# A short convolution with k as the stationary operand, and the second half of a fused kernel brought into one written-out order

## The chip, the cores and the metric

The kernel runs on one core of one Trainium2 chip. The metric is the device time of one execution in microseconds, the median of several runs. Lower is better.

## The reference

The input `A_q` (2048 x 640, time by channels) passes through two blocks with residuals, both conditioned by `c`. Cut to what matters:

```python
def _A_ref(q, k, v, shift_k, ssm_k, ssm_D):          # 2048 x 640, ks = 4
    k_pad = jnp.pad(k, ((0, 0), (ks - 1, 0), (0, 0)))
    for t in range(ks):                              # short convolution, per channel
        k_shift = k_shift + k_pad[:, t:t + S, :] * shift_k[:, ks - 1 - t]
    kv = k_shift * v
    y = irfft(rfft(kv, 2 * S) * rfft(ssm_k, 2 * S))[:S]   # long convolution, per channel
    return q * (y + kv * ssm_D)

def _B_ref(x, w_in, w_sp, b_sp, w_out):              # Fh = 864
    z = gelu(x @ w_in)                               # 2048 x 1728
    z1, z2 = z[..., :Fh], layernorm(z[..., Fh:])
    g = w_sp @ z2 + b_sp                             # w_sp mixes over time, 2048 x 2048
    return (z1 * g) @ w_out

sa, ca, ga, sb, cb, gb = split(silu(c) @ w_mod)      # 6 x 640
x = x + ga * _A_ref(layernorm(x) * (1 + ca) + sa, k, v, ...)
x = x + gb * _B_ref(layernorm(x) * (1 + cb) + sb, ...)
```

## The kernel before

Data and matrices are bf16, sums in PSUM are fp32. There are 16 time tiles of 128 rows and five "units" of 128 channels each.

**Short convolution** (`load_kv`, `short_conv`, L512 to L559). For each unit the DMA brings k and v transposed, channels on the partitions and time along the row (`big`, 128 x 4096). `dg` holds four 128 x 128 diagonal matrices with the four taps. `taps` runs 16 matmuls per unit, all at L245: `dg` is stationary, 512 columns of k, shifted by 0 to 3, move. `times_v` (L553, DVE) multiplies the PSUM tile `sm` by v in place. `kvw` (L559, on SP's queue) writes the unit's 512 KB into a DRAM scratch array `kv_scr`, and `load_X` (L390) reads it back in the layout that the transform wants: the 16 time blocks times 8 channels of a group on the partitions. This is the tile `X` of the input side (XU). The filter `ssm_k` comes into the same layout straight from DRAM (XK), and DVE adds `ssm_D` to one column of it (L400).

**Long convolution.** It is a transform by matmuls. Per unit: stage 1 multiplies `X` by a small table `F1bd`; ACT or DVE casts the result to X1 (L248); `forward` multiplies by `M`; DVE multiplies input and filter spectra (`Tf` or `T`, L462), POOL or DVE adds the real and imaginary products (`W`, L476); `inv` multiplies by `G`; the casts `Z<-pz` follow; a transfer turns Z (`ZT<-Z`, L685); a last small stage with `Ebd` gives y, which is multiplied by the normed x (`gh`, L678) and added to `xt` (L698). The layer norm of x takes its statistics on DVE (L580) or on ACT (L576, L577) and is applied on DVE, ACT or POOL (L606 to L610).

**gMLP.** Norm and modulation of the new x (Z, L843 to L897), z = gelu(x w_in) by 320 matmuls of 432 columns, then the spatial mix. It treats time tiles p and p+8 as a pair (p = 0..7). Each pair takes seven block products (`ps`, L1013) of 8 matmuls x 432 columns instead of eight. Their stationary sides are blocks of w_sp (`wT`) or sums of these (`S`, L988, DVE). DVE and ACT add them up into two tiles u (L1030 to L1047; `keep` on ACT, L1019 and L1021). Each u is turned by a DMA (`uT<-u`, L1052). `project_pair` (L1181 to L1225) multiplies a pair of uT by `w_o` in the same seven-block way: 25 matmuls of 320 columns in pieces (L1179), with sums of uT (`R`, POOL, L1171) and of w_o (`V`, L1161 and L1235), and partial rows `O` that ACT copies and POOL and DVE add up. `project` (L1140) does one tile directly with 14 matmuls.

**What sets the order.** Each engine works through its own list in program order; nothing is scheduled on the chip. Up to the first mix pair (p = 0) the program is a plan: the code registers operations with their dependences (`Plan.op`), and the string `ORDER` gives the order in which they are issued and which engine takes each where there is a choice ("D0 D13 ... S88 A1 P1032": engine letter and operation number). `SLOTS` gives the number of buffers of each pool tag. `FILLS` and `MODE` are further tables of it. After the plan the rest is issued as the code is written, in the loop over p = 1..7 (L1237): the products of pair p, with the projection of pair p-1 put between and behind them in four parts (`begin`, `most`, `sums`, `end`). Pairs 0 to 6 go through `project_pair`; tiles 7 and 15 go through `project` at the very end. SP issues nearly all DMAs, in order: when one of them has to wait for its data, all behind it wait too.

## Time and profile before

| quantity | value |
|---|---|
| median of 3 runs | 311.58 us (310.77 to 313.09) |
| profiled execution, its own time | 310.85 us |
| its span, first to last instruction | 309.1 us |
| granted TensorE clock | 1.00 throughout |
| PE busy | 293.9 us (95%), 2485 matmuls |
| DVE busy | 270.7 us (88%) |
| ACT / POOL busy | 166.6 us (54%) / 181.2 us (59%) |
| DMA | 45.23 MB, queue 1 at 68.1% of 16 engines |

The span has two stages. Up to about 133 us runs the plan's transform stage, where all engines and the DMA are busy at once; the first modulation `Z<-s` of the gMLP input on DVE (L871) starts at 133.03 us and the first matmul of z at 133.48 us. From there PE does z, the mix and the projection. "Busy" counts an engine's instructions without the time it waits; PE's matmuls are pipelined, so that the duration of one (346 ns at 432 columns) is longer than the distance from one to the next. A row of the view of groups reads: line, engine, operation, output and inputs, shapes, count, then busy us and mean ns of one, then the idle time of the engine just before them with what ended it.

### The profile page before, as it was taken

What the parts mean: (1) busy time and instruction counts of PE and PEld (TensorE: products, weight loads), DVE (VectorE), ACT (ScalarE), POOL (GpSimd) and SP (SyncE); (2) the same over time, 40 slices, a digit from 0 to 9 for tenths busy, and PEclk for the clock granted to TensorE, in tenths of its full rate; (3) what the DMA queues carried; (4) which work ended last, traced back from release to release, by engine and by line L of the source; (5) the groups of instructions that cost most, each with busy time, mean ns of one, the idle gap of its engine ahead of it and who ended that gap; (6) DMA issues with size and microseconds to landing.
All of it is one profiled execution on the core that took longest, in us unless ns stands there. A gap on an engine that the chain in (4) does not pass through costs nothing.

```text
span 309.1 us, 6509 instructions
## 1 busy us (share of the span) xinstructions
PE 293.9 (95%) x2485; PEld 195.3 (63%) x2485; DVE 270.7 (88%) x523; ACT 166.6 (54%) x302; POOL 181.2 (59%) x208
## 2 busy tenths in 40 slices
PE   7988989989999998989999999999999999999995
PEld 2765678867889998645555555555555555565554
DVE  8898998979998988998897998998999878888574
ACT  6988699978888957547676688141111111021110
POOL 2542877838988999555423612039858475673922
PEclk9999999999999999999999999999999999999999
DMA  8999899998995849404679910073477593730323
GB/s 177 210 227 253 231 305 224 220 190 196 225 223 113 203 84 298 152 2 95 127 146 237 204 3 0 2 127 70 89 152 165 120 192 73 167 81 21 83 55 111
DMA packets 127954, 45.23 MB, mean 146 GB/s; under 512 B 117071, under 2 KB 127156, under 8 KB 127924
## 3 DMA queue, kind: packets, MB, share of 16 engines
q1 hardware_dynamic: 127770, 44.78, 68.1%
q8 instruction: 19, 0.31, 0.4%
q14 instruction: 11, 0.09, 0.1%
q10 hardware_dynamic: 154, 0.05, 0.1%
HBM read 16.11 MB, written 5.24 MB: 69 GB/s over the span
## 4 chain that ended last, share of the span: by engine, by line
PE 47%; DVE 12%; issue 1%; POOL 1%; DMA 1%; ACT 1%; DVEq 0%; POOLq 0%
PE ps L1013 21%; PE pu L245 8%; PE pz L245 8%; PE po L1179 6%; DVE st L704 2%; PE pz L1013 1%; PE po L1140 1%; DVE Tf L462 1%; DMA uT<-u 1%; DVE T L462 1%; DVE xt L698 1%; PE pu L1013 1%; DVE u L1041 1%; DVE T L998 1%; DVE gh L746 1%
## 5 line engine op out<-in xcount | busy, mean ns | idle before, releaser
L245 PEld LDWEIGHTS <-Z 128*128 128x128 bf16 x320 | 31.2, 98 | 28.1 <-DVE Z L871 1.3
L245 PE MATMUL pu<-X,M 128*128 128x128 bf16 (+1 forms) x480 | 45.8, 237 | 2.3 <-DVE Tf L462 1.9
L245 PEld LDWEIGHTS <-M 128*128 128x128 bf16 x480 | 37.4, 98 | 8.8 <-issue 3.2
L476 POOL TENSOR_TENSOR W<-Tf 128x256 bf16<-128x256 f32 x47 | 34.7, 760 | 11.6 <-DVE Tf L462 8.3
L1013 PEld LDWEIGHTS <-S 128*128 128x128 bf16 x256 | 25.0, 98 | 21.6 <-issue 0.5
L245 PE MATMUL pz<-big,Z 128*128 128x432 bf16 x160 | 33.1, 346 | 0.8 <-DVE Z L871 0.8
L248 ACT CAST X<-s 128x1024 bf16<-128x1024 f32 x31 | 31.9, 1028 | 2.5 <-PE s L245 2.3
L245 PE MATMUL pu<-big,Z 128*128 128x432 bf16 x160 | 32.5, 346 | 0.0
L462 DVE TENSOR_TENSOR Tf<-pu,KH 128x1024 f32<-128x1024 f32 x25 | 30.3, 1219 | 2.4 <-PE pu L245 1.2
L1197 ACT COPY O<-po 128x320 f32<-128x320 f32 x7 | 3.0, 427 | 54.4 <-PE po L1179 54.4
L1013 PEld LDWEIGHTS <-wT 128*128 128x128 bf16 x192 | 18.8, 98 | 16.6 <-issue 1.0
L245 PEld LDWEIGHTS <-G 128*128 128x128 bf16 x330 | 24.7, 98 | 2.0 <-issue 0.2
L248 ACT CAST KH<-pu 128x512 bf16<-128x512 f32 x40 | 23.0, 600 | 5.1 <-PE pu L245 5.1
L248 ACT CAST Z<-pz 128x512 bf16<-128x512 f32 x38 | 22.3, 601 | 5.3 <-PE pz L245 5.1
L245 PEld LDWEIGHTS <-X 128*128 128x128 bf16 x288 | 18.1, 97 | 7.6 <-DMA X<-kv_scr 2.3
L1013 PE MATMUL ps<-X,wT 128*128 128x432 bf16 x112 | 22.7, 346 | 0.0
L1013 PE MATMUL ps<-T,S 128*128 128x432 bf16 x112 | 22.7, 346 | 0.0
L1200 POOL TENSOR_TENSOR O<-O,xt 128x320 f32<-128x320 f32 x7 | 6.4, 908 | 27.7 <-ACT O L1199 27.7
L1013 PE MATMUL ps<-X,S 128*128 128x432 bf16 x112 | 21.6, 346 | 0.0
L245 PE MATMUL s<-F1bd,X 128*128 128x256 bf16 x128 | 19.2, 272 | 2.2 <-DVE X L400 1.2
L245 PE MATMUL sm<-big,dg 128*128 128x512 bf16 (+1 forms) x80 | 20.4, 379 | 0.0
L926 DVE BATCH_NORM_STATS2 stz<-X 128x6 f32<-128x432 bf16 x32 | 18.1, 591 | 0.9 <-ACT X L920 0.7
(205 smaller groups left out, 664.3 us busy)
## 6 DMA issues: line engine op xcount, KB each, us to landing
wm<-in_w_mod_dram SPq DMA_DIRECT2D x6, 800.0 KB, 6.0
xt<-in_A_q_dram SPq DMA_DIRECT2D x4, 640.0 KB, 6.2
out_dram<-ot SPq DMA_DIRECT2D x15, 160.0 KB, 2.4
big<-in_B_w_in_dram SPq DMA_DIRECT2D x2, 1080.0 KB, 9.2
X<-in_A_ssm_k_dram SPq DMA_DIRECT2D x4, 512.0 KB, 5.2
kv_scr<-big SPq DMA_DIRECT2D x4, 512.0 KB, 3.5
X<-kv_scr SPq DMA_DIRECT2D x4, 512.0 KB, 4.8
w_o<-in_B_w_out_dram SPq DMA_DIRECT2D x6, 160.0 KB, 3.1
```

Of the source, the lines that this page charges most:

```text
L245: nc.tensor.matmul(o, lhsT=w, rhs=x, start=start, stop=stop)
L248: (e.copy if e is nc.scalar else e.tensor_copy)(dst, src)
L462: e.tensor_tensor(T_[:], (tl[pu] if src is None else tl[src])[:, :, :, None, :].to_broadcast(shape), tl[KH][:, :, None, :, :].to_broadcast ...
L476: e.tensor_tensor(tl[W][:, :, o, :], T_[:, :, 0, o, :], T_[:, :, 1, 1 - o, :], op=ALU.add if o else ALU.subtract)
L698: op("GD" if u < NU - 1 else "D", "res", lambda e: e.tensor_tensor(sl, sl, gl, op=ALU.add), r=[("gh", (u, g))], w=[("xt", (u, n)) for n in ...
L704: op("D", "ln2", lambda e, n=n: e.bn_stats(out=st2[:, n, (0, 0, 0, 1, 2)[u], :], in_=xt[:, n, us[0] * DU:(u + 1) * DU]), r=[("xt", (v, n)) ...
L746: op("D", "yml", lambda e, ghv=ghv, py=py, i0=i0, k=k: e.tensor_tensor(ghv, ghv, tl[py][:, i0:i0 + k], op=ALU.mult), r=[py], w=[("gh", (u, ...
L926: op("D", "stz", lambda e, i=i, n=n, fc=fc: e.bn_stats(out=stz[:, n, fc, :], in_=tl[z2][:, i, fc * FC:(fc + 1) * FC]), r=[(z2, (i, fc))], ...
L998: nc.vector.tensor_tensor(y if o is None else T[o][:, sl, :], x, y, op=ALU.subtract)
L1013: nc.tensor.matmul(ps[:, :FC], lhsT=lhs[:, s_, :], rhs=rhs(s_), start=(s_ == 0 and not more), stop=(s_ == HT - 1), skip_group_check=more)
L1179: nc.tensor.matmul(ps[:, :HS], lhsT=w(k), rhs=x(k), start=start and k == 0, stop=stop and k == n - 1, skip_group_check=True)
L1200: nc.gpsimd.tensor_tensor(m5, m5, x_of(1, 1), op=ALU.add)
```

## The change

Two things change at once, with one new `ORDER` for everything.

*Short convolution.* k still comes transposed, now with 16 columns of zeros ahead of it (`KPAD`, a memset). The operands change places: a 128-column slice of k, shifted by 0 to 3, is stationary, and a 128 x 128 `dg` moves. The result has time on the partitions and channels along the row. A unit takes 16 x 4 = 64 matmuls of 128 columns instead of 16 of 512; that makes 320 in place of 80. v is loaded as it lies in DRAM, without a transpose: unit 0 alone in two halves, then units 1 and 2 as one transfer of 1 MB, then 3 and 4. `times_v` (now L610) writes to a new tile in Z's pool, in the order (c n g). One transposing transfer from SBUF to SBUF (`regroup`, L625) turns that into XU. The scratch array in DRAM, its six writes and its six reads are gone. XU's rows come in another order (n, g), so stage 1 gets a second table `F1ng` for it, with one more small mask, one more set of index bits, and one more cosine on ACT.

*The rest in the plan.* Everything behind the first mix pair is now registered in the plan as well (1438 operations in `ORDER`). The sums S, V, R and O and the multiplications by z1 (`lsm`, `c22b`, `c22m`) may stand on DVE or POOL; some u multiplications thus go to POOL. `c22` and `last_sum` are split into separate operations. `PAIRS` is (1, ..., 6): tiles 0 and 8 are projected directly, with 28 matmuls instead of 25 and without R and O for that pair. Pieces of the projection and products of later pairs alternate piece by piece. `SLOTS` is extended by the tags of the mix.

```diff
 FILLS = (4, 6, 2, 2, 4, 3, )
+PAIRS = (1, 2, 3, 4, 5, 6)
-SLOTS = dict(Tf=2, W=2, X=3, X1=4, KH=9, T=3, Z=3, ZT=1, wm=1, big=2, dg=2, st1=2, s1=1, sm=2, pu=2, pz=2)
+SLOTS = dict(Tf=2, W=2, X=3, X1=4, KH=9, T=3, Z=3, ZT=1, wm=1, big=2, dg=2, st1=2, s1=1, sm=2, pu=2, pz=2,
+             wT=6, S0=2, S1=2, S2=2, S3=2, mm=4, o=4, m1=1, m5=1, ms=1, c22=1, c=1, u0=2, u1=2, uT=4, R=2, ot=3,
+             O0=1, O1=1, O2=1, O3=1, O4=1, O5=1)
-D0 D13 D100 G101 S88 A1 P1032 P7 A4 A10 G5 A23 D15 D102 D109 D103 D110 A112 D115 A111 S2 D6 P1033 P8 A11 D14 A16 D116
+G5 D13 D101 D0 D14 A1 G102 S525 D103 S2 D116 D15 P7 A10 S23 D104 S83 S84 S26 G122 D117 G6 A4 P1034 A38 S24 D18 A532 P8
...
-                        mm(ps[i // k][:, i % k, :], tl[X][:, cp + i, :], F1flat, True, True)
+                        mm(ps[i // k][:, i % k, :], tl[X][:, cp + i, :], F1flat[X[1]], True, True)
...
-        SCH = 512
-                e.dma_start_transpose(tl[name][:, o + h * m:o + (h + 1) * m], src[0, h * m:(h + 1) * m, dt * P:(dt + 1) * P])
+        KPAD = 16
+        SCH = 4
+        GROUP = {0: (0,), 1: (1, 2), 3: (3, 4)}
+                    e.dma_start_transpose(k_of(u)[:, KPAD + h * m:KPAD + (h + 1) * m], A_k[0, h * m:(h + 1) * m, u * DU:(u + 1) * DU])
+            op("DG", "kpad", lambda e: e.memset(k_of(u)[:, 0:KPAD], 0.0), r=[(name, "new")], w=[(name, ("k", j, "pad"))])
+                    e.dma_start(v_of(0, ns.start, NT // n) if u0 == 0 else tl[name][:], v_nat[:, ns, ds])
...
-                    p_ = new(ps, "sm", [P, SCH], F32)
-                    for j in range(4):
-                        lo = 0 if i else j
-                        mm(p_[:, lo:], tl[dg][:, j, :], tl[name][:, i * SCH - j + lo:(i + 1) * SCH - j], j == 0, j == 3)
+                    p_ = new(ps, "sm", [P, SCH, DU], F32)
+                    for m in range(SCH):
+                        t0 = KPAD + (i * SCH + m) * P
+                        for j in range(4):
+                            mm(p_[:, m, :], k_of(u)[:, t0 - j:t0 - j + P], tl[dg][:, j, :], j == 0, j == 3)
...
-                    e.tensor_tensor(vsl, tl[ps][:], vsl, op=ALU.mult)
+                    dst = tl[kvt][:].rearrange("p c (n g) -> p n c g", g=8)[:, i * SCH:(i + 1) * SCH]
+                    e.tensor_tensor(dst, tl[ps][:].rearrange("p n (c g) -> p n c g", g=8),
+                                    v_of(u, i * SCH, SCH).rearrange("p n (c g) -> p n c g", g=8), op=ALU.mult)
...
-                op("S", "kvw", lambda e, sl=sl: e.dma_start(kv_scr[dt * P:(dt + 1) * P, sl],
-                                                                   tl[name][:, S + sl.start:S + sl.stop]),
+                    e.dma_start_transpose(tl[name][:, cs, :], tl[kvt][:, cs, :].rearrange("p c q -> p (c q)"))
+                op("S", "kvt", fn, r=[kvt] + ([(name, "new")] if h else []), w=[(name, h)] + ([] if h else [(name, "new")]),
...
-                late("D", "lastsum", lambda: last_sum(0, "d", 0, 1), r=["paird", "s1", "bcol", ("z1", (0, 1))], w=[("u", 0)])
+                    late("D", "lsa", lambda e: last_sum(e, p, "d", 0), r=[pair["d"], s1_, "bcol"], w=["cd_%d" % p], new=[("cd_%d" % p, "c")])
+                    late("DG", "lsm", lambda e: last_sum(e, p, "d", 1), r=["cd_%d" % p, ("z1", (p, 1)), (U[0], "new")], w=[(U[0], 1)])
...
-    for p in range(1, HT):
-        nxt = p + 1 < HT
-        product(p, 1, bank)
...
-    project(HT - 1)
-    end()
-    project(NT - 1)
+        for p in range(HT):
+            if p in PAIRS:
+                project_pair(p)
+            else:
+                project(p)
+                project(p + HT)
+        plan.run({"P": nc.tensor, "A": nc.scalar, "D": nc.vector, "G": nc.gpsimd, "S": nc.sync})
```

The order moves instructions on every engine. Three places follow. In the rows the number at the end of a name counts tiles and differs between the two kernels.

First, SP's queue in the first quarter of the program (`xt` is a part of x, `wm` of w_mod). Before:

```order
9 L566 DMA xt_68<-in_A_q_dram 128x4x640
10 L521 DMA_TRANSPOSE big_334<-in_A_k_dram 128x2048
11 L559 DMA kv_scr_134<-big_207 128x1024 x2
12 L754 DMA KH_385<-in_c_dram 5x128
13 L521 DMA_TRANSPOSE big_334<-in_A_v_dram 128x2048
14 L390 DMA X_483<-kv_scr_134 128x8x128 x2
15 L566 DMA xt_68<-in_A_q_dram 128x4x640
16 L521 DMA_TRANSPOSE big_575<-in_A_k_dram 128x2048
17 L521 DMA_TRANSPOSE big_575<-in_A_v_dram 128x2048
18 L559 DMA kv_scr_134<-big_334 128x2048
```

After:

```order
8 L820 DMA KH_243<-in_c_dram 5x128
9 L632 DMA xt_66<-in_A_q_dram 128x4x640
10 L417 DMA X_383<-in_A_ssm_k_dram 128x16x128
11 L625 DMA_TRANSPOSE X_414<-Z_284 128x8x128 x2
12 L564 DMA_TRANSPOSE big_492<-in_A_k_dram 128x2048
13 L632 DMA xt_66<-in_A_q_dram 128x4x640
14 L579 DMA ZT_531<-in_A_v_dram 128x16x256
15 L564 DMA_TRANSPOSE big_492<-in_A_k_dram 128x2048
16 L632 DMA xt_66<-in_A_q_dram 128x4x640
17 L686 DMA wm_664<-in_w_mod_dram 128x5x640
18 L625 DMA_TRANSPOSE X_854<-Z_593 128x16x128
```

The write and read of the scratch array (rows 11 and 14, then 18) became one row per unit, the transposing regroup (rows 11 and 18); v's transposing loads became plain ones, and the loads of x moved relative to them.

Second, the start of ACT's list (`gh` and `sums` are the layer norm's statistics of x, `M2` the forward matrix, `X1` the cast of the first stage). Before:

```order
4 L248 COPY sk_102<-sm_158 128x4x5
5 L536 ACTIVATE dg_167<-ident_73,sk_102 128x128 x4
6 L348 ACTIVATE M2_80<-T_174,mturn_125 128x4x64 x2
7 L248 CAST D_col_101<-sm_196 128x80
8 L255 ACTIVATE f1c_122<-f1i_123,mpi_118 128x32
9 L348 ACTIVATE M2_80<-T_182,mturn_125 128x4x64 x2
10 L348 ACTIVATE M2_80<-T_177,mturn_125 128x4x64 x2
11 L248 CAST X1_238<-pz_239 128x2x32x8
```

After:

```order
6 L591 ACTIVATE dg_190<-ident_71,sk_101 128x128 x4
7 L642 ACTIVATE gh_93,sums_108<-xt_66 128x640
8 L643 ACTIVATE gh_93,sums_108<-xt_66 128x640
9 L272 CAST D_col_100<-sm_206 128x80
10 L375 ACTIVATE M2_78<-T_158,mturn_125 128x4x64 x2
11 L279 ACTIVATE f1c_122<-f1i_123,mpi_118 128x32
12 L642 ACTIVATE gh_93,sums_108<-xt_66 128x640
13 L643 ACTIVATE gh_93,sums_108<-xt_66 128x640
14 L375 ACTIVATE M2_78<-T_177,mturn_125 128x4x64 x2
15 L272 CAST X1_259<-pz_260 128x2x32x8
```

Two tiles' statistics of x now stand ahead of the first cast of X1, the first of them ahead of the sines for M2.

Third, the end of DVE's list (`u2`, `u3` are the last pair's u, tiles 7 and 15; L1142, and L1310 after, close the direct projection of a tile). Before:

```order
443 L1041 TENSOR_TENSOR u3_2791<-c22_4325,G2_81 128x432
444 L1046 SCALAR_TENSOR_TENSOR c_4343<-ps_4279,bcol_2787,s1_4314 128x432
445 L1047 TENSOR_TENSOR u2_2790<-c_4343,G2_81 128x432
446 L1046 SCALAR_TENSOR_TENSOR c_4356<-ps_4316,bcol_2787,s1_4314 128x432
447 L1047 TENSOR_TENSOR u3_2791<-c_4356,G2_81 128x432
448 L1204 TENSOR_TENSOR O_3422<-po_4333,O_3422 128x320
449 L1212 TENSOR_TENSOR ot_4329<-po_4331,xt_68 128x320
450 L1217 TENSOR_TENSOR ot_4330<-po_4334,O_3422 128x320
451 L1218 TENSOR_TENSOR ot_4329<-po_4332,O_3422 128x320
452 L1142 TENSOR_TENSOR ot_4393<-po_4394,xt_68 128x320
```

After:

```order
433 L1122 SCALAR_TENSOR_TENSOR c_4582<-ps_4510,bcol_3033,s1_4508 128x432
434 L1124 TENSOR_TENSOR u2_3036<-c_4582,G2_79 128x432
435 L1122 SCALAR_TENSOR_TENSOR c_4593<-ps_4541,bcol_3033,s1_4508 128x432
436 L1350 TENSOR_TENSOR ot_4567<-po_4521,O_3919 128x320
437 L1344 TENSOR_TENSOR O_3919<-po_4595,O_3919 128x320
438 L1344 TENSOR_TENSOR O_3919<-O_3919 128x320
439 L1350 TENSOR_TENSOR ot_4615<-po_4610,O_3919 128x320
440 L1350 TENSOR_TENSOR ot_4617<-po_4577,xt_66 128x320
441 L1350 TENSOR_TENSOR ot_4617<-po_4550,O_3919 128x320
442 L1350 TENSOR_TENSOR ot_4615<-po_4610,O_3919 128x320
443 L1310 TENSOR_TENSOR ot_4666<-po_4639,xt_66 128x320
```

The two multiplications that finish u3 have left DVE for POOL, and the last pair projection is closed entirely behind the last product's sums; on PE 26 matmuls of pairs 5 and 6 now stand between the last product and tile 7.

665 lines of the change are left out of this document (378 added, 287 removed).

## Prediction

> **What bounds the kernel now.** I read the table of windows first, cut where the program changes its nature: at 133 us, where the gMLP's input begins, and at 205 us, where the mix from pair 1 on begins. Its columns are busy us and count for PE, PEld, DVE, ACT and POOL, then the granted clock, the DMA share and GB/s.
>
> ```profile
> 0.00:133.00 133.00, 123.71 (x1497) 99.74 (x1497) 120.82 (x225) 107.51 (x192) 92.20 (x118) 1.00 0.93 205
> 133.00:205.00 72.00, 70.70 (x390) 37.63 (x391) 65.35 (x170) 44.99 (x83) 23.90 (x31) 1.00 0.48 93
> 205.00:309.00 104.00, 99.44 (x600) 57.96 (x598) 84.50 (x130) 14.10 (x29) 65.09 (x60) 1.00 0.52 108
> ```
>
> The clock is full everywhere, so it explains nothing. In the first stage PE (123.7 of 133 us) and DVE (120.8) are both nearly full and feed each other; DMA is at 0.93. The stage can be shortened by about 9 us at most without taking work from PE. Behind 133 us PE alone sets the pace, and there only its gaps can be won. Next come the waits of DVE and PE, and those of SP's queue (us in total, times, longest):
>
> ```profile
> DVE X L400 <- DMA X<-in_A_ssm_k_dram: 1.9, 1, 1.9
> DVE st L580 <- DMA xt<-in_A_q_dram: 1.0, 1, 1.0
> DVE X L248 <- PE pz L245: 0.7, 1, 0.7
> DVE big L553 <- DMA big<-in_A_v_dram: 0.3, 1, 0.3
> ...
> PE pz L245 <- DMA X<-kv_scr: 1.5, 1, 1.5
> ...
> SPq L390 <- DMA kv_scr<-big: 9.3, 4, 3.7
> ```
>
> DVE's waits for loads are 1.9, 1.0 and 0.3 us. Its wait of 0.7 us for `pz` is one for a load too: that first-stage result was late because PE had waited 1.5 us for the read of the scratch array. Together they are 3.9 us of DVE's 12.2 idle us in this stage. The last row is the round trip at work: the read stands in SP's queue until the write has landed, 9.3 us in all, and every load behind it is late by that. The late `ssm_k` load is one that stands in this queue.
>
> **The taps.** Four starts of PE rows give the distance from one matmul to the next, two for 512 columns with `dg` stationary, two for 128 columns with a stationary of their own each:
>
> ```profile
> 24.45 1.03 PE L245 MATMUL sm<-big,dg 128*128 128x512 bf16 x4
> 25.32 0.38 PE L245 MATMUL pz<-F1bd,X 128*128 128x256 bf16 x2
> ...
> 123.20 0.61 PE L721 MATMUL pu<-ident,Z 128*128 128x128 bf16 x8
> 123.65 0.61 PE L721 MATMUL pz<-ident,Z 128*128 128x128 bf16 x8
> ```
>
> At 512 columns it is 0.87/4 = 217 ns, at 128 it is 0.45/8 = 56 ns. 80 x 217 = 17.4 us go and 320 x 56 = 17.9 us come: +0.5 us of PE in a stage where PE is idle for 9.3 us, so nothing on the path. The risk is the weight load, of which there are now 320 in place of 80. One lasts 98 ns, longer than the matmul that it belongs to:
>
> ```profile
> L245 PEld LDWEIGHTS <-M 128*128 128x128 bf16 x480 | 37.4, 98 | 8.8 <-issue 3.2
> ...
> 63.53 1.05 PE L245 MATMUL pu<-X,M 128*128 128x256 bf16 x12
> 64.41 0.60 PE L245 MATMUL s<-F1bd,X 128*128 128x256 bf16 x4
> ```
>
> But twelve matmuls, eight of 128 and four of 256 columns, each with a load of its own, take 0.88 us from start to start: with 98 ns each they could not be under 1.18 us. The loads overlap, and the stream runs at the rate of its columns. So the cost is between +0.5 us (56 ns) and +14 us (320 x 98 = 31.4 us against 17.4); I take +0.5, since two rows of this form stand there.
>
> The Trainium skill speaks against this. Its page "TensorE: Matmul & The Clock Gate", section "Back-to-back issue gap", gives for a long stream of pairs of weight load and matmul about 81 ns at 128 columns and 131 ns at 512, and calls the 56 ns that of an isolated matmul. By it the taps would go from 10.5 us to 25.9 us, +15 us of PE. This trace agrees with neither figure (56 and 217 ns), though no row has 16 such matmuls on odd column offsets of the stationary.
>
> **The regroup.** It takes the place of a write, a wait and a read. Median us from issue to landing:
>
> ```profile
> kv_scr<-big SPq DMA_DIRECT2D x4, 512.0 KB, 3.5
> X<-kv_scr SPq DMA_DIRECT2D x4, 512.0 KB, 4.8
> ...
> uT<-u SPq DMA_TRANSPOSE x16, 3.0
> ...
> ZT<-Z SPq DMA_TRANSPOSE x4, 8.3
> ```
>
> Write and read take 8.3 us. The trace has no transposing SBUF transfer of this size; the nearest are uT (7 blocks of 128 columns, 3.0 us) and ZT (32 blocks, 8.3 us). With 16 blocks the regroup lies between them, by blocks at 3.0 + 9 x 0.21 = 4.9 us. XU is thus there some 3.4 us earlier after its last multiplication by v, between 0 and 5.3 us, and SP is free of the blocked read. I take the 3.9 us of DVE's waits as gone; the bounds are 0 (they come back as other waits) and 3.9.
>
> **DVE's and POOL's work in the first stage.** The multiplication by v now reads v from another tile and writes in strides; its rows and those of the work that the order moves onto DVE or off it:
>
> ```profile
> L553 DVE TENSOR_TENSOR big<-sm,big 128x512 bf16<-128x512 f32 x20 | 13.4, 684 | 1.0 <-PE sm L245 0.6 <-DMA big<-in_A_v_dram 0.3
> ...
> L1041 DVE TENSOR_TENSOR u<-c,G 128x432 bf16<-128x432 f32 x8 | 6.5, 818 | 0.3
> ...
> L248 DVE CAST Z<-pz 128x512 bf16<-128x512 f32 x2 | 1.4, 676 | 0.0
> L476 DVE TENSOR_TENSOR W<-Tf 128x256 bf16<-128x256 f32 x3 | 1.3, 441 | 0.1
> L580 DVE BATCH_NORM_STATS2 st<-xt 128x6 f32<-128x320 bf16 x16 | 6.9, 472 | 1.0 <-DMA xt<-in_A_q_dram 1.0
> L610 DVE TENSOR_SCALAR gh<-xt,mv,rstd 128x640 bf16<-128x640 bf16 x4 | 2.3, 599 | 0.0
> ```
>
> The cast to Z writes a transposed order too and takes 676 ns, as the multiplication before: I take 684 again, +0. The slowest row of two operands with an fp32 source, 818 ns for 432 columns (L1041), would make it 970 ns, +5.7 us over 20. By the order DVE gains four casts to Z (2.7 us) and four sums W (1.8), and loses four statistics (1.9) and three applications of the norm (1.8): +0.8 us. What DVE loses goes to ACT and POOL, which have 25 and 41 us idle in this stage; the second F1 table and the zero columns are a few tenths on engines that wait at the start anyway.
>
> **ACT's start.** Here the order costs something. Rows of before, and what the moved statistics last (L576 and L577 are two instructions per tile, 738 ns each):
>
> ```profile
> 4.03 1.28 ACT L536 ACTIVATE dg<-ident,sk 128x128 bf16<-128x128 bf16 x4
> ...
> 8.64 0.59 ACT L248 CAST X<-pz 128x512 bf16<-128x512 f32 x1
> ...
> L576 ACT ACTIVATE gh<-xt 128x640 bf16<-128x640 bf16 x8 | 5.9, 738 | 2.5 <-DMA xt<-in_A_q_dram 2.5
> ...
> xt<-in_A_q_dram SPq DMA_DIRECT2D x4, 640.0 KB, 6.2
> ...
> 0.72 0.46 SPq L390 DMA_DIRECT2D X<-in_A_ssm_k_dram  x1
> ```
>
> The first load of x is now SP's first, in the place of the last row, and lands at about 0.7 + 6.2 = 6.9 us; ACT, whose taps matrices are done at 5.3, waits 1.6 us for it, and then works through two tiles' statistics (4 x 0.738 = 2.9 us) ahead of the first cast of X1. That cast moves from 8.64 to about 13 us, +4.4. Queued behind it are the sines of `M`, the other casts, and `KH`, for which the first product waits. DVE has index work, statistics and multiplications by v to do meanwhile, so the cost is between 0 and +4.4 us; I take +2.5.
>
> First stage: -3.9 + 2.5 + 0.8 = **-0.6 us**.
>
> **The second half.** PE's gaps behind 133 us: in the windows at the top it lacks 1.3 us up to 205 and 4.6 behind that. Of these 4.6 the last 2.9 are the end, when PE is done and the output is written. So 3.0 us of gaps are to be won. The largest that the timeline shows, and the transfer that the last one waits for:
>
> ```profile
> 222.58 0.70 PE L1179 MATMUL po<-V,uT 128*128 128x320 bf16 x4 [0.44 <-DVE ot L1217]
> ...
> 228.38 1.62 PE L1013 MATMUL ps<-T,wT 128*128 128x432 bf16 x8 [0.71 <-DVE c L1039]
> ...
> 301.64 2.08 PE L1140 MATMUL po<-w_o,uT 128*128 128x320 bf16 x14 [0.61 <-DMA uT<-u]
> ...
> 230.00 2.86 PE po L1179 x21
> ...
> 243.63 2.86 PE po L1179 x21
> ...
> 298.62 2.98 DMA uT<-u
> ...
> L1206 POOL TENSOR_TENSOR O<-O,xt 128x320 f32<-128x320 f32 x7 | 8.2, 1178 | 0.0
> L1200 POOL TENSOR_TENSOR O<-O,xt 128x320 f32<-128x320 f32 x7 | 6.4, 908 | 27.7 <-ACT O L1199 27.7
> ```
>
> The 0.44 us belongs to pair 0's projection, which came late because POOL first had to make V; now pair 0 takes no V at all, and V has the round of a pair (243.63 - 230.00 = 13.6 us) more. The 0.71 us is DVE's, behind sums S that may now go to POOL. The 0.61 us is the end: the turned u of tile 7 takes 2.98 us, and before only the 21 pieces of pair 6 (2.86 us, so 0.136 each) covered it. Now 26 pieces lie between the last product and tile 7, 26 x 0.136 = 3.5 us, and 14 x 0.136 = 1.9 more ahead of tile 15, whose u is finished on POOL (0.9 to 1.2 us by the two rows) before its 3 us of transfer. These three go: -1.8. Of the 1.3 us lost while z starts I take half as won, -0.6, since DVE sheds sums and multiplications to POOL. Tiles 0 and 8 cost 28 matmuls instead of 25, 3 x 0.136 = +0.4. Pieces and products alternate more finely; the 21 pieces change their operands five times in 2.86 us and still run at 0.136, so that costs 0. Second half: **-2.0 us**, between -2.6 (no gap left) and +0.4.
>
> **Sum.** Against the profiled execution: 310.85 - 0.6 - 2.0 = 308.25, so **308.2 us**, with a span of 306.5. The profiled execution lies 0.7 us below the median of 311.58 and close to the fastest of the runs (310.77 to 313.09); I don't add that.
>
> **Rivals.**
>
> *The round trip was hidden anyway.* DVE's work in the first stage is the same (+0.8 us), and each wait taken away comes back a little later as one for PE, ACT or a buffer. For it: only 3.9 of 12.2 idle us are waits for loads. Against it: the longest of DVE's waits (1.9 us) is one of them. Then the first stage costs +0.8 to +3.3 and the second half gives 2.0: 309.7 to 312.2, about 310.9. Chance 0.21.
>
> *Most gaps of both halves go.* All 3.9 us go, ACT's start is covered by DVE's other work, some 2.5 of the other 8.3 idle us go with it, and the second half loses all its gaps: 310.85 - 3.9 + 0.8 - 2.5 - 2.6 = 302.7. For it: POOL and ACT have room, and the order now reaches across what was fixed code. Against it: PE's own 123.7 us leave little. Chance 0.27.
>
> *The weight loads of k show (slower).* Place: the 20 groups of taps in the first stage. At 98 ns each PE gets 14 us more work and reaches 137.7 us, above the 133 that the stage lasts. PE's slack is 9.3 us, so the loads set the stage from 56 + 9300/320 = 85 ns per matmul. At 98 ns, with half of PE's present 9.3 us of waits left, the stage takes 142.3, and the kernel 310.85 + 9.3 - 2.0 = 318.2. For it: the load's own 98 ns. Against it: the row of twelve in 0.88 us. Chance 0.08. With the 81 ns of the page of the Trainium skill named above the same sum gives 132.2 + 4.6 = 136.8 and 312.7 us; the trace's 56 ns and the twelve matmuls speak against that as well, and it has no more than 0.03 of the 0.08.
>
> *POOL ends the chain (slower).* Place: every pair of the mix, where u of the upper tile now takes up to three operations on POOL, 0.9 to 1.2 us each, behind R and O sums in POOL's queue. It decides when that queue and the 3.0 us of transfer exceed the round of a pair, 13.6 us; then PE waits about 1 us in each of six pairs, and the gains of this half don't come: 310.85 - 0.6 + 0.4 + 6 = 316.7. Against it: POOL has 39 us idle of 104 there. Chance 0.12.
>
> **How the numbers follow.** My forecast, 306.5 to 310, has 0.32. A measurement of this kernel can tell about 1% from no change: below 308.5 is faster, above 314.7 slower. Faster: 0.20 of my forecast and 0.27 of the second rival, 0.47. Same: 0.12 and 0.21, 0.33. Slower: 0.08 and 0.12, 0.20. The range reaches down past the case with few gaps, to 301.5, and up to 314.5, which takes in the sum with the larger bound for v's multiplication (308.2 + 5.7 = 313.9) and leaves out most of the slower ones. The likeliest case's own range is 306.5 to 310.
>
> **What would show it.** Right: taps at 56 to 60 ns from start to start; regroup transfers at 4 to 6 us; no wait of PE or DVE for X at the first units; the first gMLP matmul at 132 to 134 us though the first X1 cast is at 12 to 14 us; no PE gap before tile 7. Wrong: taps rows at 80 ns or more; multiplications by v at 0.8 us or more; POOL as the releaser of PE in the mix; the first gMLP matmul behind 136 us or ahead of 130.

## The result and the profile after

The change makes the kernel slightly slower: 311.65 us median against 310.35 of the kernel before in the same series, a ratio of 1.0066 with the 95% interval [1.0042, 1.0091]. The forecast was 308.2 us, 2.6 below the profiled execution of before; the range of 301.5 to 314.5 holds the result, but the time went the other way. The profiled execution has a span of 309.9 us where before it was 309.1, so the profiles show 0.8 of the 1.3 us.

The windows of the kernel after, at the cuts of the prediction (busy us and count of PE, PEld, DVE, ACT and POOL, then granted clock, DMA share, GB/s):

```profile
0.00:133.00 133.00, 124.18 (x1732) 109.87 (x1733) 124.47 (x227) 104.96 (x190) 103.61 (x131) 1.00 0.87 186
133.00:205.00 72.00, 69.27 (x388) 36.94 (x385) 61.17 (x155) 46.10 (x86) 39.10 (x40) 1.00 0.44 88
205.00:310.00 105.00, 101.22 (x613) 59.28 (x611) 80.69 (x129) 12.91 (x27) 64.59 (x56) 1.00 0.52 111
```

In the first stage DVE's idle time fell from 12.2 to 8.5 us, but its work rose from 120.8 to 124.5, and POOL's from 92.2 to 103.6. PE's work behind 133 us is not shorter (170.5 us against 170.1).

The transfers and taps came as forecast. DMA issues of the kernel after (count, median us from issue to landing):

```profile
big<-in_A_k_dram SPq DMA_TRANSPOSE x6, 4.7
X<-Z SPq DMA_TRANSPOSE x6, 4.4
```

Starts of PE in the kernel after (start, duration, operation, and in brackets the idle time before it and what ended it):

```profile
6.41 1.89 PE L269 MATMUL sm<-dg,big 128*128 128x128 bf16 x16
8.09 1.91 PE L269 MATMUL s<-ident 128*128 128x512 bf16 x4
...
10.45 1.06 PE L269 MATMUL sm<-dg,big 128*128 128x128 bf16 x16
11.34 0.59 PE L269 MATMUL s<-ident 128*128 128x512 bf16 x2
...
12.65 1.95 PE L269 MATMUL sm<-dg,big 128*128 128x128 bf16 x32
14.66 0.61 PE L397 MATMUL sm<-ident,M 128*128 128x128 bf16 x8
...
18.28 0.60 PE L269 MATMUL pu<-X,M 128*128 128x256 bf16 x6 [1.07 <-DVE X L272]
```

At 10.45 us sixteen taps take 0.89 us from start to start, 56 ns each; the first sixteen take 1.68 us, 105 ns each. The last row is a cost that I had placed on ACT: the first product of the filter's chain starts at 18.28 us. Before it was 14.04:

```profile
14.04 1.04 PE L245 MATMUL pu<-X,M 128*128 128x256 bf16 x12
```

The first gMLP matmul starts at 133.78 us, before at 133.48.

DVE's and PE's waits for transfers that this change touches, in the kernel after up to 134 us (total, times, longest):

```profile
DVE Z L610 <- DMA ZT<-in_A_v_dram: 0.4, 1, 0.4
```

```profile
PE pz L269 <- DMA X<-Z: 0.2, 1, 0.2
```

Of 3.9 us of load waits on DVE 0.4 are left, and PE's 1.5 us for the scratch array have become 0.2 for the transfer. What the change was costed to remove is removed.

### The profile page after: what moved, and what is told of

It reads as the page before. It is cut to its first block, busy times and chain, and to the rows that moved or that the text cites. A ratio compares the mean times of both kernels' runs of the same rounds, so it can differ in the third digit from the quotient of the medians.

```text
span 309.9 us, 6954 instructions
## 1 busy us (share of the span) xinstructions
PE 294.7 (95%) x2728; PEld 206.1 (67%) x2728; DVE 266.3 (86%) x510; ACT 164.0 (53%) x301; POOL 207.3 (67%) x225
## 4 chain that ended last, share of the span: by engine, by line
PE 66%; DVE 11%; DMA 10%; POOL 8%; SPq 2%; issue 1%; ACT 0%; POOLq 0%; DVEq 0%
PE ps L1082 23%; PE pu L269 11%; PE pz L269 9%; PE sm L269 7%; PE po L1291 6%; PE s L269 4%; DMA big<-in_A_k_dram 4%; DMA ZT<-Z 3%; PE po L1304 2%; DMA Z<-Z 2%; PE pz L1082 2%; DVE st L770 2%; POOL xt L764 1%; PE pu L1082 1%; DMA bsp<-in_B_b_sp_dram 1%
## 5 line engine op out<-in xcount | busy, mean ns | idle before, releaser
L503 POOL TENSOR_TENSOR W<-Tf 128x256 bf16<-128x256 f32 x43 | 32.0, 761 | 8.3 <-PE pz L269 3.6
L272 ACT CAST X<-s 128x1024 bf16<-128x1024 f32 x30 | 30.6, 1020 | 6.8 <-PE s L269 6.6
L1356 ACT COPY O<-po 128x320 f32<-128x320 f32 x12 | 5.0, 427 | 43.4 <-PE po L1291 26.0
L272 ACT CAST Z<-pz 128x512 bf16<-128x512 f32 x34 | 20.1, 598 | 7.4 <-PE pz L269 7.3
L1082 PE MATMUL ps<-X,S 128*128 128x432 bf16 x112 | 22.6, 346 | 0.0
L269 PE MATMUL sm<-dg,big 128*128 128x128 bf16 x320 | 21.6, 224 | 0.4 <-DMA big<-in_A_k_dram 0.4
L269 PEld LDWEIGHTS <-big 128*128 128x128 bf16 x320 | 19.4, 100 | 1.0 <-DMA big<-in_A_k_dram 0.6
L489 DVE TENSOR_TENSOR T<-pu,KH 128x1024 bf16<-128x1024 f32 x15 | 18.1, 1215 | 0.5 <-PE pu L269 0.4
```

Of the source, the lines that this page charges most:

```text
L269: nc.tensor.matmul(o, lhsT=w, rhs=x, start=start, stop=stop)
L272: (e.copy if e is nc.scalar else e.tensor_copy)(dst, src)
L489: e.tensor_tensor(T_[:], (tl[pu] if src is None else tl[src])[:, :, :, None, :].to_broadcast(shape), tl[KH][:, :, None, :, :].to_broadcast ...
L503: e.tensor_tensor(tl[W][:, :, o, :], T_[:, :, 0, o, :], T_[:, :, 1, 1 - o, :], op=ALU.add if o else ALU.subtract)
L1082: nc.tensor.matmul(ps[:, :FC], lhsT=lhs[:, s_, :], rhs=rhs(s_), start=(s_ == 0 and not more), stop=(s_ == HT - 1), skip_group_check=more)
L1356: late("A", "ok", lambda e: e.copy(rows(i), po[p, b][:, :HS]), r=[o[b]], w=[O[i]], new=[(O[i], "O%d" % i)])
```

## The experiments

Every ratio is to the kernel before on the same chip. The changed kernel itself stood at 1.0066 and, in a second series, at 1.0078; differences between two variants are read from these.

**1. The new order's parts: turn and tail apart.** First the changed kernel once more, then two exchanges: before's order everywhere around the turned convolution, and before's order in one half only.

> The changed kernel once more, on the chip on which the next three run. Both theories: about 1 us slower than before (ratio 1.003 to 1.008), DVE's operation Z at 175 us again stretched to over 3 us while PE waits some 2 us for it.

> The turned short convolution and the regroup, with all operations in the order of before (tail with pair 0 in seven pieces, sums on the engines of before; v comes one unit at a time). Theory A (the loss comes from the new order, not from the turned convolution): PE gets 0.5 us more, the waits for the round trip (2.6 us) go in part, time 308.5 to 310, 0.5 to 1.5 us below before. Theory B (the turned convolution costs time itself: 240 more weight loads, a transposing transfer): 311 to 313, 1 us or more above before.

> The changed kernel with its new order up to the first pair of the mix, and the order of before behind it (loop over pairs, pair 0 in seven pieces, sums on the engines of before). Theory A: the new first stage and the stretched operation at 175 us stay, and the three gaps of the old tail come back (1.8 us less 0.4): 312.5 to 313.5, 1 to 2 us above the changed kernel. Theory B (the new tail is what costs): below the changed kernel, 310 to 311.

> The turned short convolution with the order of before up to the first pair of the mix, and the new order behind it (tiles 0 and 8 direct, pieces and products alternating, sums on DVE or POOL). Theory A: as the kernel with the turned convolution alone, and the gaps of the tail gone: 307 to 309, 2 to 3 us below the changed kernel. Theory B (the turned convolution costs, the order is neutral): 311 to 312, as the changed kernel.

The edits against the changed kernel (the tables of the order aside):

```diff
-PAIRS = (1, 2, 3, 4, 5, 6)
+PAIRS = (0, 1, 2, 3, 4, 5, 6)          # old_tail, turn_only
-        GROUP = {0: (0,), 1: (1, 2), 3: (3, 4)}
+        GROUP = {u: (u,) for u in range(NU)}   # turn_only, old_stage
-                        new(kvt, "Z", [P, DU // 8, P])
+                        new(kvt, KVT[u], [P, DU // 8, P])   # KVT = ZT x4, Z
```

Measured: 312.01 us for the repeat (1.0078 [1.0044, 1.0112]), 320.35 for `turn_only` (1.0353 [1.0314, 1.0393]), 313.97 for `old_tail` (1.014 [1.0092, 1.0187]), 322.25 for `old_stage` (1.0413 [1.0365, 1.0461]). So the new tail is worth about 2 us beside the new first stage (1.014 against 1.0078, with intervals that just overlap), which is the sign that I forecast for it. Beside before's first stage it is worth nothing: 1.0413 for `old_stage` against 1.0353 for `turn_only`. The turned convolution does not fit before's order: with one buffer for the product DVE waits for the transfer that empties it (row of `turn_only`):

```profile
DVE ZT L607 <- DMA X<-ZT: 4.8, 1, 4.8
```

A second pair gave the product two buffers:

> As the kernel with the turned convolution in the order of before, but the tile that the multiplication by v writes has two halves used in turn (units 0 to 3) and a tile of its own (unit 4), so that no multiplication waits for a regroup or for Z. Theory A (the turn itself is near neutral, the 10 us were waits of DVE for the one buffer, 4.8 and 6.8 us): 308.5 to 311. Theory B (the turn costs by itself, in PE's weight loads or in the transfers): 314 or more.

> The same first stage with the new order behind the first pair of the mix. Theory A (the new tail is worth the three gaps less the direct pair): 1 to 2 us below the kernel with the turn and two buffers. Theory B (the new tail brings nothing, since POOL's operations stretch DVE's): equal or above.

```diff
-                        new(kvt, KVT[u], [P, DU // 8, P])
+                        if u == 0:
+                            new("kvt", "ZT", [P, 2, DU // 8, P])
+                        if u < 4:
+                            tl[kvt] = tl["kvt"][:, u % 2]
+                        else:
+                            new(kvt, "big", [P, DU // 8, P])
```

319.43 us (1.0263 [1.0227, 1.0299]) and 320.08 (1.0281 [1.0247, 1.0315]), so the new tail gains nothing here either. What remained is SP's queue, in which the regroup waits for DVE (its products, `ZT` L611, and its multiplications of spectra, `T` L491) and ZT's transfer stands behind it (`turn_two_buffers`, SP's waits and then PE's):

```profile
SPq L626 <- DVE T L491: 12.0, 3, 6.5
...
SPq L626 <- DVE ZT L611: 8.8, 1, 8.8
```

```profile
PE sm L271 <- DMA ZT<-Z: 4.9, 1, 4.9
```

These four runs show that the turn needs its own order and buffers. They do not show what the turn costs by itself, since the waits are those of the combination.

**2. The shorter way alone.** In the kernel before, one plain transfer in place of write and read; in the kernel after, write and read in place of the transfer.

> The kernel before, with one thing changed: the products of an SBUF tile go to the X tile by one plain SBUF transfer where before they were written to the scratch array and read back (128 x 2048 bf16, no wait for a write). It leaves out the regrouping, so the values that follow are others; every other instruction and its order stay. Theory A (the shorter way is worth time, as I predicted): DVE's waits for loads of 3.9 us fall under 1.5 us, DVE's idle time of the first stage falls from 12.2 us by 2 or more, and the time falls by 2 us or more (ratio 0.994 or less). Theory B (the round trip was hidden anyway): the waits come back as others, DVE's idle time stays at 11 us or more, ratio between 0.996 and 1.004.

> The changed kernel, with each of its six regrouping transfers replaced by a write to a scratch array in DRAM and a read of it, in the place of the transfer in SP's queue: the round trip of before in the order of the change. It leaves out the regrouping, so the values that follow are others. Write and read took 8.3 us before against 4.4 us of the transfer. Theory A (the shorter way is worth time): X comes about 4 us later each time and the loads behind it too; the time is 3 us or more above the changed kernel (above 314.5 where that has 311.7; ratio above 1.015). Theory B (hidden anyway): within 1 us of the changed kernel, ratio 1.003 to 1.011.

```diff
-op("S", "kvw", lambda e, sl=sl: e.dma_start(kv_scr[...], tl[name][...]), ...)
+op("S", "kvw", lambda e, sl=sl: None, ...)
-e.dma_start(tl[name][:, cs, :], src[...])
+e.dma_start(tl[name][:, cs, :], src[...] if name[1] == "K" else tl["kv%d" % u][:, S:]...[:, cs, :])
```

```diff
-e.dma_start_transpose(tl[name][:, cs, :], tl[kvt][:, cs, :].rearrange("p c q -> p (c q)"))
+e.dma_start(rows.rearrange("r (a x) -> (r a) x", a=parts), tl[kvt][:, cs, :].rearrange("p c q -> p (c q)"))
+e.dma_start(tl[name][:, cs, :], rows.rearrange("(c g) (n f) -> (g n) c f", g=8, f=P))
```

306.61 us for `one_hop`, ratio 0.9832 [0.9801, 0.9863], and 323.08 for `two_hops`, 1.0356 [1.0315, 1.0397]. The second theory, that the round trip was hidden, falls in both orders: by the ratios it is worth 5 us in the old one and about 9 in the new. (The profiled execution of `two_hops` took 329.69 us where its median is 323.08; its rows are not used.) So the term that I had at -3.9 us was there, and something else in the change ate it.

To see what, I cut the first stage anew: at 20 us, at the first transposition of the last unit's result, and at the first gMLP matmul. Kernel before:

```profile
0.00:20.00 20.00, 18.35 (x139) 11.51 (x140) 17.17 (x57) 16.95 (x35) 8.97 (x22) 1.00 1.06 198
20.00:122.51 102.51, 95.79 (x1158) 80.49 (x1155) 93.84 (x144) 85.07 (x150) 76.23 (x90) 1.00 0.96 212
122.51:133.48 10.97, 9.57 (x204) 7.76 (x204) 10.29 (x28) 5.52 (x8) 7.49 (x8) 1.00 0.42 147
133.48:309.10 175.62, 170.14 (x988) 95.58 (x988) 149.37 (x297) 59.05 (x110) 88.52 (x91) 1.00 0.50 102
```

`one_hop`:

```profile
0.00:20.00 20.00, 18.02 (x134) 11.13 (x135) 16.71 (x55) 16.71 (x35) 8.36 (x22) 1.00 0.96 187
20.00:119.15 99.15, 95.95 (x1162) 81.01 (x1160) 94.06 (x146) 85.49 (x150) 76.65 (x90) 1.00 0.82 195
119.15:130.12 10.97, 9.56 (x203) 7.75 (x204) 10.28 (x28) 5.52 (x8) 7.47 (x8) 1.00 0.43 151
```

The kernel after:

```profile
0.00:20.00 20.00, 15.49 (x127) 10.05 (x128) 17.46 (x56) 18.00 (x43) 12.31 (x26) 1.00 1.01 198
20.00:124.07 104.07, 101.11 (x1421) 93.14 (x1420) 98.78 (x148) 81.25 (x140) 84.01 (x97) 1.00 0.91 199
124.07:133.78 9.71, 8.33 (x192) 7.17 (x193) 9.01 (x28) 5.76 (x8) 8.06 (x9) 1.00 0.01 2
133.78:309.90 176.12, 169.75 (x993) 95.74 (x990) 141.07 (x282) 58.95 (x111) 102.91 (x95) 1.00 0.49 102
```

In the long second row PE is idle for 6.7 us before, for 3.2 with one hop and for 3.0 in the change; DVE for 8.7, 5.1 and 5.3. So the change has as little idle time there as the kernel with one hop. But in that row it does 5.3 us more on PE than before (101.11 against 95.79) and 4.9 more on DVE. To the end of this row the books of PE are: 3.8 us less PE idle behind 20 us, 2.9 more ahead of it, 2.5 more PE work in all, together +1.6 us (124.07 against 122.51); the short third row gives 1.3 back, and 0.3 is left. Counted on DVE, the same +1.6 us is 0.3 us less idle time ahead of 20 us, 3.4 less behind it, and 5.2 us more work. Books like these do not say which engine caused it.

How the 2.9 and 2.5 divide differs between executions with the same start: in experiment 3's run PE's work to this point is 0.5 us above that of before, and its idle time in the first 20 us 4.2 above. Part of PE's work are 18 matmuls that only fill (`s<-ident`) where before had 14, and the sixteen taps at 105 ns. The sums vary less, +5.3 and +4.7 us.

**3. A gap of 2.1 us in the second half.** PE's gaps of the kernel after behind 133 us, then DVE and POOL around 175 us:

```profile
142.49 2.00 PE L269 MATMUL pz<-big,Z 128*128 128x432 bf16 x10 [0.55 <-DVE Z L941]
...
178.57 2.00 PE L269 MATMUL pu<-big,Z 128*128 128x432 bf16 x10 [2.14 <-DVE Z L967]
...
302.49 0.70 PE L1291 MATMUL po<-V,uT 128*128 128x320 bf16 x4 [0.81 <-DVE ot L1350]
```

```profile
171.94 0.75 DVE L967 TENSOR_SCALAR Z<-Z,cb_col,sb_col 128x512 bf16<-128x512 bf16 x1 [0.68 <-PE pz L269]
...
174.95 3.56 DVE L967 TENSOR_SCALAR Z<-Z,cb_col,sb_col 128x512 bf16<-128x512 bf16 x1
```

```profile
174.76 1.51 POOL L1159 TENSOR_TENSOR w_o<-w_o,gb_bf 96x640 bf16<-96x640 bf16 x1
176.24 2.11 POOL L1057 TENSOR_TENSOR S<-wT,S 128x1024 bf16<-128x1024 bf16 x1
```

The same DVE operation takes 0.75 us and then 3.56: it starts 0.2 us after a POOL operation and ends 0.16 us after the second of two is over. The repeat of the changed kernel has the gap again, 2.29 us. In the kernel before, DVE did all sums S and all multiplications of `w_o` by `gb` itself, and its own modulations of Z around the same time were short:

```profile
172.13 0.40 DVE L897 TENSOR_SCALAR Z<-Z,cb_col,sb_col 128x512 bf16<-128x512 bf16 x1
...
174.20 0.35 DVE L897 TENSOR_SCALAR Z<-Z,cb_col,sb_col 128x512 bf16<-128x512 bf16 x1
```

I moved the one long operation to POOL's queue, ahead of the two:

> The changed kernel with one of the 15 modulations of Z moved from DVE to POOL, ahead of the two sums that POOL did meanwhile. Theory A (DVE's operation was held up by POOL's sums and PE waited 2.1 us for it): 1.5 to 2.1 us below the changed kernel, about 310. Theory B (the wait would have come at the next modulation or cast anyway): no change.

```diff
-... D979 G980 A981 ... P934 D978 D933 ...
+... D979 G980 G978 A981 ... P934 D933 ...
```

310.85 us, ratio 0.9992 [0.9964, 1.0021]. The gap is gone (PE of that run, 15 matmuls and then the next ten without a pause):

```profile
173.14 2.90 PE L269 MATMUL pz<-big,Z 128*128 128x432 bf16 x15
175.88 1.99 PE L269 MATMUL pu<-big,Z 128*128 128x432 bf16 x10
```

One operation out of 1438 table entries takes back the whole loss of 0.7% by the ratios. The span shrinks by less than the gap, from 309.9 to 309.0 us, since two other waits of PE come up behind it:

```profile
192.56 1.07 PE L269 MATMUL pu<-big,Z 128*128 128x432 bf16 x5 [0.46 <-ACT G L990]
...
196.49 0.89 PE L1082 MATMUL pu<-X,wT 128*128 128x432 bf16 x4 [0.67 <-ACT X L1011]
```

So theory A holds for the operation and its gap, and a part of theory B for the time. The Trainium skill's page "SBUF — State Buffer", section "Who interferes with whom", says that VectorE and GpSimd share one pair of SBUF ports as an exclusive lock, and that, for VectorE's modes that use both its port pairs, the one that comes second is blocked for the other's whole instruction, not slowed. The rows agree: 3.40 us were left of both POOL operations when DVE's started, and it took 3.56 us, not 0.75 us at half speed.

**4. POOL's load and DVE's.** DVE's operations on SBUF tiles had become longer in the first stage, those with a PSUM source had not (by form, mean ns behind the comma; W was 441 ns before). Kernel before, then kernel after:

```profile
L661 DVE TENSOR_TENSOR gh<-gh,gca_bf 128x512 bf16<-128x512 bf16 x10 | 4.3, 451 | 0.0
...
L661 DVE TENSOR_TENSOR gh<-gh,gsa_bf 128x512 bf16<-128x512 bf16 x8 | 3.1, 419 | 0.1
```

```profile
L727 DVE TENSOR_TENSOR gh<-gh,gca_bf 128x512 bf16<-128x512 bf16 x10 | 5.0, 513 | 0.0
...
L503 DVE TENSOR_TENSOR W<-Tf 128x256 bf16<-128x256 f32 x7 | 4.2, 605 | 0.1
...
L727 DVE TENSOR_TENSOR gh<-gh,gsa_bf 128x512 bf16<-128x512 bf16 x7 | 3.9, 555 | 0.0
```

> The changed kernel without the 23 modulations of gh that POOL does in the first stage (27.3 us of POOL there; those on DVE stay). It leaves out that part of the computation. Theory A (an operation on POOL lengthens DVE's operations on SBUF tiles, which is what made DVE's work 3.1 us longer than before): the means fall back to those of before or under them, W from 605 to 450 ns or less, gh by gca from 513 to 460 or less, gh by gsa from 555 to 430 or less, while operations with a PSUM source stay at 1217 and 679 ns; DVE's busy time up to 133 us falls by 2.5 us or more. Theory B (the means rose because other instances went to DVE): the means of the same forms stay within 5%. The time: by A 2 to 4 us less than the changed kernel, since DVE feeds PE in this stage; by B less than 1 us.

```diff
-            o["fn"](engines[e])
+            if not (e == "G" and o["kind"] == "ghm"): o["fn"](engines[e])
```

```profile
L727 DVE TENSOR_TENSOR gh<-gh,gca_bf 128x512 bf16<-128x512 bf16 x10 | 4.1, 428 | 0.0
...
L503 DVE TENSOR_TENSOR W<-Tf 128x256 bf16<-128x256 f32 x7 | 3.9, 563 | 0.1
...
L727 DVE TENSOR_TENSOR gh<-gh,gsa_bf 128x512 bf16<-128x512 bf16 x7 | 2.9, 411 | 0.0
```

311.08 us, 0.9992 [0.9962, 1.0022]. The modulations fall as theory A says, W only by 7%: the stretching is shown for the first two and is a part of W's at most. Single rows of the kernel after agree: operations of these three forms beside an idle POOL took 0.41 us, and the longest, 1.27 us at 78.94 us, had POOL busy all the while. DVE's work up to 133 us falls by 2.2 us, a little less than theory A's 2.5. But the first gMLP matmul does not move (133.96 against 133.78 us); the time came from the second half, where the gap of experiment 3 was 1.4 us in this run. The next run took work from DVE in another way:

> The changed kernel with the one modulation on POOL of the earlier run, and further four casts of the middle of the first stage (one of X1, 1.21 us, three of Z, 0.68 us each) on ACT in place of DVE, at the same place of the order, where ACT has 15 to 43% idle, and the third modulation of the first gMLP tiles ahead of two statistics on DVE instead of behind them. Theory A (DVE's load holds the first stage): DVE's work there falls by 3 us, the gap of 0.47 us at 142 us goes, and the time is 0.5 to 2 us under that of the earlier run, 309 to 310.3, under the kernel before. Theory B (DVE's time saved comes back as waits, because PE's products come no earlier): 310.5 to 311.

```diff
-D291 D269 D353 D403 (casts of the first stage), ... D756 ... D780 ...
+A291 A269 A353 A403, ... D780 D756 ...
```

311.59 us, 1.0004 [0.9977, 1.0031], no better than experiment 3. DVE's busy time fell, and the stage did not:

```profile
20.00:123.83 103.83, 101.13 (x1422) 93.29 (x1419) 96.85 (x143) 83.42 (x144) 84.17 (x97) 1.00 0.91 200
```

1.9 us less on DVE than in the change, 0.2 us earlier. The gap at 142 us went, and PE waited as much for ACT later.

**5. The start.** Four runs moved work in the first 20 to 40 us or made it lighter.

> The changed kernel with four tiles' statistics on ACT moved behind the casts of X1 and the first casts of KH. Theory A of the prediction (ACT's start costs 2.5 us, up to 4.4): 1 to 3 us below the changed kernel, the first X1 cast at 8 to 9 us. Theory B (the start is hidden, since PE and DVE then wait for the first k and the regroup): no change, or a loss where gh and ln wait.

> The changed kernel with the one modulation on POOL of the earlier run (310.85 us), and its first 20 us in another order, nothing else: the taps matrices of unit 0 on POOL in place of ACT, the sine of the first F1 table ahead of the first statistics on ACT and its table ahead of a small operation on DVE, the third tile's statistics on ACT behind three casts of X1, and on DVE one cast of X1 ahead of the first statistics and of the second F1 table. Theory A (the start costs what the shorter way gives): the first F1 product starts about 1 us earlier than 9.80 us, the first product with M at 15.5 to 16.5 us in place of 18.28, the first gMLP matmul 1.5 to 2.5 us earlier than 133.8, and the time is 308.5 to 310. Theory B (DVE and POOL later in the stage set its length): the time stays at 310.5 to 311.5.

> As early_k, and the kernel's own load (the first half of ssm_k's unit 0) is SP's first again as it was before, the first load of x comes sixth, and the first two statistics of ACT stand behind the second and third cast of X1. Theory A: the first F1 product at 8.2 to 8.8 us, the first product with M at 14.5 to 16, the time 307.5 to 309.5, under early_k. Theory B: 310.5 to 312, since ACT's statistics then fall into the casts of the next units, as in the run with all four moved.

> The changed kernel with every statistic of x on ACT taken over 16 of its 640 columns (ten tiles, two activations each; it leaves out the other columns' share in the norm's mean and variance), so that some 0.5 us of each of the twenty go and nothing moves: about 4 us less on ACT ahead of 18.5 us, 10 us in all. Theory A (ACT's work at the start holds the kernel's chain back): the first product with M at 15 to 16.5 us, the first gMLP matmul 2 us or more earlier than 133.8, the time 307.5 to 309.7 where the changed kernel has 311.7 to 312. Theory B (ACT does not hold it, DVE and POOL do): within 0.7 us of the changed kernel.

```diff
-A10 ... D117 G6 A4 P1034 A38 ... D123 ... A16 ... A153 A534 ... D528 P149 ... A151 D150
+A10 G38 ... D117 G6 A4 A16 P1034 ... D17 D123 ... A153 ... P149 D150 D528 ... A151 A534     (early_k, on experiment 3's kernel)
-A1 G102 S525 D103 S2 ... S23 D104 S83 S84 S26 ... A532 ... A533
+A1 S83 S2 G102 D103 ... D104 S23 S84 S26 S525 ... A148 A532 ... A153 A533                   (early_k2, on early_k)
-e.activation(gh[:, n, :], xt[:, n, :], ACT.Copy, accum_out=...)
+e.activation(gh[:, n, 0:16], xt[:, n, 0:16], ACT.Copy, accum_out=...)                       (short_stats; Square too)
```

(`stats_later` moves A532 to A535 and D536 behind the casts of X1 and KH, with no other edit.) 316.27 us (1.0169 [1.013, 1.0209]), 311.91 (1.0022 [0.9999, 1.0045]), 313.23 (1.0096 [1.0059, 1.0133]) and 311.49 (1.0029 [1.0007, 1.0052]). In `short_stats` ACT has 10 us less to do up to 133 us, 3.7 of them ahead of 18.5 us; the first product with M still starts at 18.09 us and the first gMLP matmul at 134.36, so my reason for the late start, ACT's statistics, is refuted. `early_k` brings that product to 16.58 us, but not PE's work: it is held up right behind it, and the first gMLP matmul comes at 133.21 us, 0.6 earlier than in the change.

```profile
16.58 0.60 PE L269 MATMUL pu<-X,M 128*128 128x256 bf16 x6
18.55 0.61 PE L269 MATMUL s<-F1bd,X 128*128 128x256 bf16 x4 [1.36 <-DVE X L427]
```

The two slower runs put the statistics into the casts of the next units, and PE then does 2 us and DVE about 3 us less than in the change between 20 and 30 us, with ACT nearly full and the granted clock at 0.83 (`stats_later`):

```profile
20.00:30.00 10.00, 7.50 (x75) 6.13 (x73) 5.95 (x13) 9.72 (x22) 2.45 (x3) 0.83 1.12 276
```

**6. Is PE the bound then?**

> The changed kernel with two of the four taps left out in units 1 to 4 (128 matmuls of 128 columns, 7.1 us of PE by 56 ns; unit 0 keeps its four; it leaves out half of those units' short convolution), nothing moved. Theory A (from 20 us on PE's own work sets the first stage): the first gMLP matmul 3 to 6 us earlier than 133.8 and the time 306 to 309. Theory B (DVE's 125 us of work set it, and PE's extra work is hidden in its gaps, as I predicted): the first gMLP matmul within 1.5 us of 133.8, the time above 310.5.

> The kernel before with the same left out: two of four taps in units 1 to 4 (32 matmuls of 512 columns, 6.9 us of PE by 217 ns). If PE has room in the stage of before because it waits for the round trip (8.4 us of gaps), the work taken away widens the gaps and the time falls by less than 2.5 us; if PE's work sets the stage there too, by 4 us or more.

> The kernel before with three places changed in SP's queue alone: the last load of x and the kernel load of unit 2 ahead of the first modulation table and, for x, of unit 1's read of the scratch array, and one modulation table between unit 3's write and its read. Nothing else moves and all is computed. Theory A (the loads behind the waiting read are a good part of what the round trip costs): DVE's wait of 1.9 us for ssm_k goes, the time falls by 1 to 2.5 us, ratio 0.992 to 0.997. Theory B (it is X itself that comes too late): ratio 0.998 to 1.003.

```diff
-mm(p_[:, m, :], k_of(u)[...], tl[dg][:, j, :], j == 0, j == 3)
+if u == 0 or j < 2: mm(p_[:, m, :], k_of(u)[...], tl[dg][:, j, :], j == 0, j == (3 if u == 0 else 1))
-S526 A542 ... S89 ... S565 ... S525 ... S91 ... S69 ... S580
+S526 S525 A542 ... S89 S91 ... S565 ... S69 S580                       (loads_first, in the order of before)
```

310.59 us for `half_taps` (1.0004 [0.9981, 1.0027]), 310.21 for `before_half_taps` (0.9987 [0.9962, 1.0012]) and 312.76 for `loads_first` (1.0066 [1.0036, 1.0096]). The long row of `half_taps`:

```profile
20.00:123.46 103.46, 95.94 (x1285) 86.03 (x1283) 98.36 (x146) 80.78 (x138) 84.10 (x97) 1.00 0.90 200
```

5.2 us less PE work, 0.6 us earlier: PE alone is not the bound either. DVE's idle time there is 5.1 us, as in `one_hop` (5.1) and in the change (5.3). So theory A fails here, and with it the plainer story that the taps ate the gain. (By the ratios the run is 0.6 to 0.7% below the changed kernel; in the profile it is 1.2 us, of which 0.6 come from the gap of experiment 3, 1.53 us long here.) In the kernel before the same cut brings the first gMLP matmul from 133.48 to 132.77 us, and the time not clearly below: PE's work was hidden there too, to about the same degree.

`loads_first` gains nothing: with these loads ahead of the waiting read PE's waits for X rise from 1.5 to 3.0 us, DVE's wait for `ssm_k` is 2.3 us where it was 1.9, and the first gMLP matmul comes at 137.55 us. (That profiled execution took 315.23 us where the median is 312.76, so a part of these 4 us is its own.) So nothing here supports the queue behind the read as a good part of what the round trip costs; other orders of the queue were not run.

## Why the prediction was wrong, point by point

The forecast took 2.6 us off the profiled execution; it became 0.8 longer. Of these 3.4 us, 2.5 lie in the second half and 0.9 in the first stage. The step that failed, and for which the runs show what came in its place, is in the second half: I counted what DVE hands to POOL as relief for DVE, at no price to what DVE keeps.

- **Second half, -2.0 us: +0.5. This step failed.** DVE did shed work, 8 us of it behind the first gMLP matmul, and the gaps of 0.44 and 0.71 us and the wait for `uT` that I named are gone; the timeline lists no gap of PE from 180 to 300 us. But two operations that had gone from DVE to POOL, a multiplication of `w_o` and a sum S, stretched one modulation on DVE to 3.56 us, and PE stood still for 2.14 us (shown by experiment 3). With that operation moved this half takes 175.4 us in place of 176.1, which is still not the forecast: waits for ACT came up. Ahead of tile 7 PE now waits 0.81 us for DVE in place of 0.61 for the transfer. Of the 0.6 us that I took as won while z starts nothing came: PE waits 0.55 us at 142 us, and before it was 0.22 and 0.33. PE's work there fell by 0.4 us, where I had +0.4 for the direct pair.
- **Taps, +0.5 us hidden:** the rate was right, 56 ns in nearly every row; the first sixteen take 105 ns each, behind a pause of PE, and those at 25.38 us 67. That they lie off the path holds in the sense that 5.2 us less PE work gains 0.6 us.
- **Regroup, 4.9 us:** 4.4. **Multiplications by v, 684 ns:** 679 and 684. **Waits, -3.9 us:** right. DVE's idle time fell by 3.7 us, and `one_hop` has nearly the same gain at the first gMLP matmul, 133.48 to 130.12 us, in the old order. The rival that the round trip was hidden is refuted; that the result lies in its range, 309.7 to 312.2, is chance.
- **DVE's work, +0.8 us: too small.** To the first gMLP matmul it is +4.0 (from 121.3 to 125.3), to the end of the units +5.2. Of these, some 2.6 us are instructions that the order added, at their prices of before; I had counted only some of them. The other half are longer operations, W and the two modulations of gh above all. I had priced each moved operation by its row of before, as if the price did not depend on POOL, which does 11 us more; without POOL's modulations DVE's work to the end of the units falls by 2.0 us.
- **The start, +2.5 us:** the place and size were near (+2.9 us of PE idle ahead of 20 us), the mechanism was not: the first statistics began at 5.51 us, not at 6.9, the first cast came at 10.59, not at 13, and ACT's statistics are not what counts.
- **First stage, -0.6 us: +0.3.** On PE it is -3.76 of idle time, +5.32 of start and PE work, -1.26 in the last part that I had not costed. What I think failed is the idea that work added to PE and DVE goes into their idle time. With the round trip gone, both have only 3 and 5 us of it left over 104 us, and taking 5.2 us of work from PE alone or 1.9 from DVE alone gained 0.6 and 0.2 us, as if each were held by the other. This is argued, not shown: in the kernel before, where PE has 6.7 us idle, the same cut of the taps gained as little at the first gMLP matmul (0.7 us).
- **POOL ends the chain:** not in the form of this rival, since PE has no wait in the mix; POOL acted through DVE, and in z.

What stays open: that both engines set the first stage together is argued from runs that took from one at a time. A kernel that takes work from both was not run, so the cause of the first stage's 0.9 us stays open. Why the filter's chain starts 4 us later is not settled either: the edits of the start that brought work forward moved the wait to another place. No version beat both kernels; the one of experiment 3 is level with the kernel before. `one_hop` is faster than both but leaves the regrouping out.
